# One reloaded factor rounded and split two places sooner at the turn of the pairs (gated linear attention and bilinear GLU, one Trainium2 core)

## The chip, the core and the metric

The kernel runs on one core of one Trainium2 chip. The metric is the device time of one execution in microseconds (us). Before the change it is 596.92 us, the median of 3 runs (596.91 to 597.69).

The engines are named as in the profile: PE multiplies matrices, PEld loads the stationary operand, DVE is VectorE, ACT is ScalarE, POOL is GpSimd, SP issues most of the transfers. Each engine runs its own instructions in the order in which the program emits them; between engines there are semaphores.

## What is computed

```python
x = A_x                                   # 2048 tokens, width 512
g = sigmoid((x * gate_w).sum(-1))
a = linear_attention(x, A_wqkv) @ A_wo    # 32 heads of 16, phi(t) = where(t > 0, t + 1, exp(t)) + 1e-6
b = ((x @ B_w_gate) * (x @ B_w_up)) @ B_w_down     # inner width 1792
return g * a + (1 - g) * b
```

All data are float32. The kernel gets that precision out of PE by splitting each operand into a rounded high part and a low part (`hi`, `lo = src - hi`) and by making three matmuls of each product: high by high, high by low, low by high. A split is one ACT instruction (the rounding copy) and one DVE instruction (the subtraction), and the DVE one waits for the ACT one.

## The kernel before

The 2048 tokens are worked in two pairs of two chunks of 512. A first phase makes the key-value sums over all tokens; then come 32 units, 16 for each pair. A unit (`unit`, line 484) takes one 128-column block of the gate and up weights (or of the query weights) and makes the two by two blocks of the result with seven products instead of eight (a Strassen-like scheme). Each product (`product`, line 502) is six matmuls: two halves of the contraction, three matmuls each. The seven products go in the order 2, 3, 4, 1, 5, 6, 7, into four PSUM banks called Y, X, R and S (`bY`, `bX`, `bR`, `bS` in the profile).

The factor of product `i` on the token side is `xc[i]`, a pair of tiles, high and low: `xc1h` and `xc1l` for product 1, a part of `xbh` and `xbl` for product 5, `xc6h` and `xc6l` for product 6, a part of `xah` and `xal` for product 7. These factors belong to a pair of chunks, so they have to be renewed between unit 15, the last of the first pair, and unit 16, the first of the second. Factors 2, 3 and 4 of the second pair are made early and kept elsewhere. Factors 1, 5, 6 and 7 are reloaded by `reload` (line 489): right after the last product of unit 15 that reads factor `i`, SP issues a 512 KB load of the summed x into the low tile, and the split of it (ACT rounds it into the high tile, DVE subtracts in place) is put off to a place of unit 16. The trace calls the ACT instruction `xc1h<-xc1l` and the DVE one `xc1l<-xc1l,xc1h`; for factor 5 they are `xbh<-xbl` and `xbl<-xbl,xbh`.

What sets the order of the work is written out by hand. A unit calls named places in between its products, in the order of `PLACES` (line 43): high, low, e, m, c, d, t, s, r, end. `later(n, place, fn)` (line 418) puts a function on the list of a place, `do(n, place)` (line 421) runs the list in the order in which it was filled. For unit 16 the stretch that matters is, in program order (lines 510 to 540):

- product 2 into Y; ACT empties Y into `m`; place high
- product 3 into X; DVE writes R from X and `m`; places low and e; the down-projection jobs of this point (none in unit 16)
- product 4 into Y; ACT empties it into `cross[0]`; places m and c; one down-projection job (six matmuls into `pdn`); place d
- the rounding of the next unit's weights (`wch`), then product 1 onto R; DVE makes `t` from R and `cross[0]`; place t
- product 5 onto X; DVE makes S from `t` and X; two jobs; place s; two jobs; product 6, place r, product 7

Before the change the splits of factors 1, 5, 6 and 7 stand at the places m, c, t and s of unit 16. At the places high and low of unit 16 the rounding and the subtraction of the last hidden tile of unit 15 are queued as well (lines 588 and 589; `xc4l<-cross` on ACT and `xc4l<-cross,xc4l` on DVE in the trace, because its buffer is a part of a tile that has become free). Line 589 is reached after `reload(1)`, so what `reload(1)` puts on the place low comes ahead of that subtraction in the list.

After the turn the order goes on without a break: attention units whose denominators take a way through DRAM (`den<-den`, `rb<-den`) and, at the end of the second pair, a second seven-product scheme for the down projection (`sa`, `sb`).

Of the kernel before, what the change touches and what calls it, by code (L numbers as in the profile page):

```python
# [42 lines left out]
PLACES = "high low e m c d t s r end".split()  # L43
# [5 lines left out]
)  # L49
STARTS = (0, 4, 5, 7)  # L50
MOST = (2, 3, 2, 2)
Q_AFTER = ((5, 9), (0, 3))


# [9 lines left out]
def gated_mix(ctx: ExitStack, tc, xt, xp, x, wqkv, wq, wq_add, wo, wgu, wgu_add, wdn, gate_w, out):  # L64
# [12 lines left out]
    def act(dst, src, func=AF.Copy, **kw):  # L77
        pin(nc.scalar.activation(dst, src, func, **kw))  # L78

    def tt(dst, a, b, op):  # L80
        pin(nc.vector.tensor_tensor(dst, a, b, op=op))  # L81
# [12 lines left out]
    def mm3(dst, lhs, rhs, start, stop, on=False, late=0, part=range(3)):  # L94

        (lh, ll), (rh, rl) = lhs, rhs
        three = ((lh, rh), (ll, rh), (lh, rl)) if late else ((lh, rh), (lh, rl), (ll, rh))
        for i in part:
            mm(dst, *three[i], start=start and i == 0, stop=stop and i == 2, skip_group_check=on)

    def dma(dst, src):
        tc.keep_in_program_order(nc.sync.dma_start(dst, src))
# [45 lines left out]
    order = []  # L148
    for pair, after in enumerate(Q_AFTER):
        for f in range(NF):  # L150
# [3 lines left out]
    units = len(order) // NPAIR  # L154
# [11 lines left out]
    def w_add(n):  # L166

        if n < len(order):
            _, kind, m = order[n]
            act(raws[n][:, 3:5], raws[n][:, 0:1].to_broadcast([P, 2, 2 * P]))  # L170
            act(raws[n][:, 5:7], raws[n][:, 0:2], scale=-1.0)
            dma_add(raws[n][:, 2:7], (wgu_add if kind == "f" else wq_add)[m])
# [3 lines left out]
    def w_high(n):  # L176
        if n < len(order):
            wcs[n] = [const.tile([P, 7, 2 * P], F32R, tag=f"wc{v}", name=f"wc{v}", bufs=2) for v in "hl"]
            for a, b in PARTS:
                act(wcs[n][0][:, a:b], raws[n][:, a:b])  # L180

    def w_low(n, part):
        if n < len(order):
            a, b = PARTS[part]
            tt(wcs[n][1][:, a:b], raws[n][:, a:b], wcs[n][0][:, a:b].bitcast(F32), ALU.subtract)
# [19 lines left out]
    with tc.tile_pool(name="p1", bufs=2, reuse_waits="tile") as p1:  # L205
# [11 lines left out]
        for t in range(2 * CH // P):  # L217
            c, i = divmod(t, CH // P)
# [180 lines left out]
    def put(*some):  # L399
        for one in some:  # L400
            if one.home:
                spare.append(one.r)
            else:
                live.remove(one)

    def two(name):
        return [Buf(name + v, True) for v in "hl"]
# [10 lines left out]
    def later(n, place, fn):  # L418
        at.setdefault((n, place), []).append(fn)

    def do(n, place):
        for fn in at.pop((n, place), []):
            fn()
        if n >= units:
            clock[0] += 1
            advance(dve=MOST[0], act=MOST[1])

# [13 lines left out]
    def advance(**most):  # L441

        for i, job in enumerate(jobs):
            for k, chain in enumerate(job.chains):
                while chain:
                    kind, lead, gap, fn, ready = chain[0]
                    if lead < i or clock[0] < job.free[k] or not ready() or not most.get(kind, 1):
                        break
                    if kind in most:
                        most[kind] -= 1  # L450
                    fn()
                    job.free[k] = clock[0] + gap
                    chain.pop(0)
# [3 lines left out]
    def down(k, all_=False):  # L457

        owed[0] += k
        for _ in range(owed[0]):  # L460
            if not jobs or jobs[0].apart and passed[0] == passed[1] and not all_:
                break
            waits = [stage for chain in jobs[0].chains for stage in chain]
            if waits and not all_:
                break
            for kind, lead, gap, fn, ready in waits:
                assert ready(), clock
                fn()
            job = jobs.pop(0)
            owed[0] -= 1  # L470
            clock[0] += 1
            job.mms()
            passed[1] = passed[0]
            advance(dve=MOST[2], act=MOST[3])
            if job.after:
                job.after()
        if not jobs:
            owed[0] = 0


    def share(n):
        return SECOND[n - units] if n >= units else FIRST[n]

    def unit(n, quad=None, sign=None, og=None):

        wh, wl = wcs.pop(n)
        bank = {t: psum.tile([P, CH], F32, tag=t, name=f"b{t}") for t in "YXRS"}

        def reload(i):
            if n + 1 == units and i not in xsum:  # L490
                spare.extend(v[:, k] for v in xc[i] for k in range(2))
            elif n + 1 == units:
                hi, lo = xc[i]
                dma(lo.bitcast(F32), xsum[i])

                def split_there():
                    act(hi, lo.bitcast(F32))
                    tt(lo, lo.bitcast(F32), hi.bitcast(F32), ALU.subtract)

                later(units, {1: "m", 5: "c", 6: "t", 7: "s"}[i], split_there)  # L500

        def product(i, to, start=False):
            for k in range(2):
                ks = slice(k * P, (k + 1) * P)
                x = [v.r for v in kept[i, k]] if n >= units and i not in xsum else [v[:, k] for v in xc[i]]
                mm3(bank[to], (wh[:, SLOT[i], ks], wl[:, SLOT[i], ks]), x, start and k == 0, k == 1, not start)
            passed[0] += 1
            reload(i)

        turned = [sign is not None and c != sign for c in range(2)]  # L510
        m2 = Buf("m2")
        product(2, "Y", True)
        act(m2.f, bank["Y"])
        do(n, "high")
        product(3, "X", True)

        tt(bank["R"], bank["X"], m2.f, ALU.subtract)
        put(m2)
        do(n, "low")
        do(n, "e")  # L520
        many = share(n)
        down(many[0])
        cross = [Buf(f"cross{c}") for c in range(2)]
        product(4, "Y")
        act(cross[0].f, bank["Y"], scale=-1.0 if turned[0] else 1.0)
        do(n, "m")
        do(n, "c")
        down(many[1])
        do(n, "d")
        if n:  # L530
            w_high(n + 1)
        w_add(n + 2)
        product(1, "R")
        t = Buf("t")
        tt(t.f, bank["R"], cross[0].f, ALU.subtract if turned[0] else ALU.add)
        if n:
            w_low(n + 1, 0)
        do(n, "t")
        product(5, "X")
        tt(bank["S"], t.f, bank["X"], ALU.subtract)  # L540
        put(t)
        act(cross[1].f, bank["X"], scale=-1.0 if turned[1] else 1.0)
        down(many[2])
        if quad:
            quad(1, 0, cross[0].f)
            put(cross[0])
        if n:
            w_low(n + 1, 1)
        do(n, "s")
        down(many[3])  # L550
        w_low(n + 1, 2)
        if quad:
            quad(0, 1, cross[1].f)
            put(cross[1])
        product(6, "R")

        def hidden(c, to):
            tt(cross[c].f, bank[to], cross[c].f, ALU.mult)
            if og and c == 0:
                tt(cross[c].f, cross[c].f, og.f, ALU.mult)  # L560

        if quad:
            quad(1, 1, bank["R"])
        else:
            hidden(1, "R")
            if sign is None:
                h = {c: two("h") for c in range(2)}
                act(h[1][0].r, cross[1].f)
        do(n, "r")
        product(7, "S")  # L570
        if quad:
            quad(0, 0, bank["S"])
            return
        if sign is not None:
            hidden(0, "S")
            return cross

        def high(c):
            act(h[c][0].r, cross[c].f)

        def low(c):
            tt(h[c][1].r, cross[c].f, h[c][0].f, ALU.subtract)
            put(cross[c])

        if n + 1 < len(order):
            hidden(0, "S")
            low(1)
            later(n + 1, "high", lambda: high(0))
            later(n + 1, "low", lambda: low(0))
        else:  # L590
            low(1)
            hidden(0, "S")
            high(0)
            low(0)
        return h
# [610 lines left out]
```

## Time and profile before

| | us |
|---|---|
| median of 3 runs | 596.92 |
| lowest and highest run | 596.91, 597.69 |
| the profiled execution, its own time | 596.23 |
| span of that execution, first to last instruction | 594.5 |
| PE busy in the span | 587.7 |

The profile is that of one execution. Busy times of the engines overlap each other. A matmul of 128x512 is shown with 0.39 us, but the matmuls are pipelined, and the next one starts some 0.23 us after it. In a timeline a row gives the start, the duration, the engine, the line, the operation, the tiles (written before the arrow, read behind it), the shape and, in brackets, the idle time of the engine before it and what ended that. Nearly all instructions are recorded at the lines of small helpers: L72 is any matmul, L78 any ACT activation, L81 any DVE operation on two tensors, L102 any load or store by SP, L105 any adding transfer by POOL. They are told apart by their tiles.

### The profile page before, as it was taken

What the parts mean: (1) busy time and instruction counts of PE and PEld (TensorE: products, weight loads), DVE (VectorE), ACT (ScalarE), POOL (GpSimd) and SP (SyncE); (2) the same over time, 40 slices, a digit from 0 to 9 for tenths busy, and PEclk for the clock granted to TensorE, in tenths of its full rate; (3) what the DMA queues carried; (4) which work ended last, traced back from release to release, by engine and by line L of the source; (5) the groups of instructions that cost most, each with busy time, mean ns of one, the idle gap of its engine ahead of it and who ended that gap; (6) DMA issues with size and microseconds to landing.
All of it is one profiled execution on the core that took longest, in us unless ns stands there. A gap on an engine that the chain in (4) does not pass through costs nothing.

```text
span 594.5 us, 7844 instructions
## 1 busy us (share of the span) xinstructions
PE 587.7 (99%) x2634; PEld 482.8 (81%) x2634; DVE 476.8 (80%) x772; ACT 348.3 (59%) x620; POOL 82.6 (14%) x103
## 2 busy tenths in 40 slices
PE   9999999999999999999999999999999999999997
PEld 6888888888888888888888788887788888888886
DVE  6877896775576788776888757996898999699996
ACT  3856775677538454663564646448957855655620
POOL 0011100100111000001110043203104202401000
PEclk9999999999999999999999999999999999999999
DMA  9477947978777967558694879769877957733003
GB/s 305 156 205 129 287 98 220 226 205 241 218 153 173 291 165 209 134 142 185 145 235 126 234 181 238 208 148 237 181 202 125 242 110 175 142 73 62 1 0 142
DMA packets 63064, 103.29 MB, mean 174 GB/s; under 512 B 8288, under 2 KB 33376, under 8 KB 63008
## 3 DMA queue, kind: packets, MB, share of 16 engines
q1 hardware_dynamic: 49568, 68.72, 35.2%
q0 software_dynamic: 13168, 33.56, 32.7%
q10 hardware_dynamic: 288, 0.52, 0.3%
q8 instruction: 20, 0.33, 0.2%
q14 instruction: 20, 0.16, 0.1%
HBM read 86.77 MB, written 16.66 MB: 174 GB/s over the span
## 4 chain that ended last, share of the span: by engine, by line
PE 96%; DMA 2%; DVE 0%; ACT 0%; issue 0%; SPq 0%; DVEq 0%
PE pdn L72 18%; PE bR L72 14%; PE bY L72 14%; PE bX L72 14%; PE pk L72 7%; PE gt L72 7%; PE bS L72 7%; PE sa L72 7%; PE sb L72 6%; DMA rb<-den 1%; PE warm L72 1%; PE pw L72 0%; PE pkv L72 0%; DMA den<-den 0%; DVE xc1l L81 0%
## 5 line engine op out<-in xcount | busy, mean ns | idle before, releaser
L81 DVE TENSOR_TENSOR wcl<-wr,wch 128x512 fp32r<-128x512 f32 (+1 forms) x96 | 73.5, 774 | 1.6 <-ACT wch L78 1.5
L81 DVE TENSOR_TENSOR acc<-pdn,acc 128x512 f32<-128x512 f32 (+1 forms) x71 | 47.4, 681 | 21.4 <-PE pdn L72 21.0
L78 ACT ACTIVATE wch<-wr 128x512 fp32r<-128x512 f32 (+1 forms) x96 | 60.3, 694 | 3.0 <-DMA wr<-in_wgu_add 3.0
L105 POOL DMA_DIRECT2D wr<-in_wgu_add x28 | 27.0, 964 | 236.6 <-ACT wr L78 149.7
L78 ACT ACTIVATE hh<-cross 128x512 fp32r<-128x512 f32 x29 | 18.2, 627 | 50.1 <-DVE cross L81 50.1
L72 PE MATMUL pdn<-hl,dh 128*128 128x512 f32 (+1 forms) x113 | 43.8, 387 | 0.0
L72 PE MATMUL pdn<-hh,dl 128*128 128x512 f32 (+1 forms) x113 | 43.7, 387 | 0.0
L72 PE MATMUL pdn<-hh,dh 128*128 128x512 f32 (+1 forms) x113 | 43.7, 387 | 0.0
L81 DVE TENSOR_TENSOR bR<-bX,m 128x512 f32<-128x512 f32 x32 | 22.3, 697 | 22.9 <-PE bX L72 22.7
L78 ACT ACTIVATE m<-bY 128x512 f32<-128x512 f32 x32 | 19.1, 598 | 36.3 <-PE bY L72 36.0
L78 ACT ACTIVATE cross<-bY 128x512 f32<-128x512 f32 x32 | 19.1, 596 | 36.2 <-PE bY L72 36.2
L72 PE MATMUL bX<-xbh,wch 128*128 128x512 f32 x96 | 37.3, 389 | 0.0
L72 PE MATMUL bX<-xbl,wch 128*128 128x512 f32 x96 | 37.3, 389 | 0.0
L72 PE MATMUL bX<-xbh,wcl 128*128 128x512 f32 x96 | 37.3, 389 | 0.0
L78 ACT ACTIVATE wr<-wr 128x512 f32<-128x512 f32 x64 | 36.5, 620 | 1.3 <-DMA wr<-in_wgu 1.3
L81 DVE TENSOR_TENSOR t<-bR,cross 128x512 f32<-128x512 f32 x32 | 22.0, 688 | 15.2 <-PE bR L72 8.5
L78 ACT ACTIVATE cross<-bX 128x512 f32<-128x512 f32 x32 | 19.0, 593 | 25.7 <-DVE bS L81 25.7
L72 PE MATMUL bR<-xc1l,wch 128*128 128x512 f32 x64 | 25.0, 391 | 0.8 <-DVE xc1l L81 0.8
L72 PE MATMUL bR<-xc1h,wch 128*128 128x512 f32 x64 | 25.2, 393 | 0.3 <-ACT xc1h L78 0.3
L72 PE MATMUL bR<-xc6h,wch 128*128 128x512 f32 x64 | 25.1, 392 | 0.0
L72 PE MATMUL bS<-xah,wch 128*128 128x512 f32 x64 | 25.0, 391 | 0.0
L72 PE MATMUL bR<-xc1h,wcl 128*128 128x512 f32 x64 | 24.9, 389 | 0.0
(385 smaller groups left out, 1732.6 us busy)
## 6 DMA issues: line engine op xcount, KB each, us to landing
wr<-in_wgu_add POOLq DMA_DIRECT2D x28, 640.0 KB, 6.9
wr<-in_wgu SPq DMA_DIRECT2D x28, 384.0 KB
xraw<-in_x SPq DMA_DIRECT2D x16, 256.0 KB
wdr<-in_wdn SPq DMA_DIRECT2D x16, 256.0 KB
terms<-zq SPq DMA_DIRECT2D x16, 256.0 KB
zt<-terms SPq DMA_DIRECT2D x16, 256.0 KB
rb<-den SPq DMA_DIRECT2D x16, 256.0 KB
ws<-in_wdn SPq DMA_DIRECT2D x30, 128.0 KB
```

The costliest lines, as they stand in the source:

```text
L72: tc.keep_in_program_order(nc.tensor.matmul(*args, **kw))
L78: pin(nc.scalar.activation(dst, src, func, **kw))
L81: pin(nc.vector.tensor_tensor(dst, a, b, op=op))
L105: tc.keep_in_program_order(nc.gpsimd.dma_start(dst, src, accum_op=ALU.add))
```

## The change

The places of the four reloaded factors are moved into a table, `RELOAD`, that gives one number for the rounding and one for the subtraction: the index of the place in `PLACES`, counted from the place high of unit 16.

```diff
+RELOAD = {1: (1, 1), 5: (4, 4), 6: (6, 6), 7: (7, 7)}
...
                 hi, lo = xc[i]
                 dma(lo.bitcast(F32), xsum[i])
 
-                def split_there():
+                def high():
                     act(hi, lo.bitcast(F32))
+
+                def low():
                     tt(lo, lo.bitcast(F32), hi.bitcast(F32), ALU.subtract)
 
-                later(units, {1: "m", 5: "c", 6: "t", 7: "s"}[i], split_there)
+                for fn, at_ in zip((high, low), RELOAD[i]):
+                    m, one = divmod(at_, len(PLACES))
+                    later(units + m, PLACES[one], fn)
```

Index 4 is c, 6 is t and 7 is s, so factors 5, 6 and 7 keep their places. Index 1 is low, where it was m (index 3): one ACT instruction and one DVE instruction, once in the kernel, stand two places sooner. No instruction, transfer or buffer is added or removed, and the load of the factor is issued at the point where it was.

## The prediction

> **What bounds the kernel now.** I read the page's head first, then the list of who waited for whom, for PE alone, over the whole span.
>
> ```profile
> span 594.5 us, 7844 instructions
> PE 587.7 (99%) x2634; PEld 482.8 (81%) x2634; DVE 476.8 (80%) x772; ACT 348.3 (59%) x620; POOL 82.6 (14%) x103
> ```
> ```profile
> PE warm L72 <- DVE xc1h L128: 1.3, 1, 1.3
> PE bR L72 <- DVE xc1l L81: 0.8, 1, 0.8
> PE sb L72 <- ACT sb L78: 0.7, 1, 0.7
> PE bR L72 <- ACT xc1h L78: 0.3, 1, 0.3
> ```
>
> PE is the bound: it works 587.7 us of 594.5, and the list holds only four waits. The one for `warm` is the start of the kernel. Two of the other three are waits of product 1 for the two halves of `xc1`, the very split that moves. Next the chain that ended last, in order of time, around the turn, and PE's own instructions there.
>
> ```profile
> 330.90 1.06 ACT xc1h L78
> ...
> 331.99 1.24 DVE xc1l L81
> ...
> 333.26 1.43 PE bR L72 x5
> 334.69 1.36 PE bX L72 x6
> ```
> ```profile
> 331.34 0.39 PE L72 MATMUL pdn<-hl,xal 128*128 128x512 f32 x1
> 332.00 0.50 PE L72 MATMUL bR<-xc1h,wch 128*128 128x512 f32 x1 [0.27 <-ACT xc1h L78]
> 333.26 0.50 PE L72 MATMUL bR<-xc1l,wch 128*128 128x512 f32 x1 [0.76 <-DVE xc1l L81]
> 333.60 0.40 PE L72 MATMUL bR<-xc1h,wcl 128*128 128x512 f32 x1
> ...
> 334.53 0.39 PE L72 MATMUL bX<-xbh,wch 128*128 128x512 f32 x1
> 334.76 0.39 PE L72 MATMUL bX<-xbl,wch 128*128 128x512 f32 x1
> 334.98 0.39 PE L72 MATMUL bX<-xbh,wcl 128*128 128x512 f32 x1
> ...
> 335.89 0.39 PE L72 MATMUL pdn<-hh,dh 128*128 128x512 f32 x1
> ```
>
> The chain leaves PE here: it runs through ACT's rounding and DVE's subtraction of `xc1` and comes back to product 1. The reader should not add up the idle times in brackets (0.27 + 0.76), for they are measured against matmuls recorded as 0.39 us long, while undisturbed ones follow each other every 1.36 / 6 = 0.227 us. From the start at 331.34 to the one at 335.89 lie 13 such steps, 2.95 us undisturbed; the trace has 4.55. **The turn costs PE 1.60 us**: 0.43 before the first matmul of product 1 (332.00 where 331.57 was due), 1.03 before the second (333.26 where 332.23 was due), and the rest after the restart, since the step from 333.26 to 333.60 is 0.34 instead of 0.227.
>
> **The change, step by step.** It adds and removes nothing; it moves two instructions. What stands where they go is in ACT's and DVE's timelines.
>
> ```profile
> 328.24 0.62 ACT L78 ACTIVATE xc4l<-cross 128x512 fp32r<-128x512 f32 x1
> 330.41 0.60 ACT L78 ACTIVATE cross<-bY 128x512 f32<-128x512 f32 x1 [1.54 <-PE bY L72]
> 330.90 1.05 ACT L78 ACTIVATE xc1h<-xc1l 128x1024 fp32r<-128x1024 f32 x1
> 331.85 1.05 ACT L78 ACTIVATE xbh<-xbl 128x1024 fp32r<-128x1024 f32 x1
> ```
> ```profile
> 329.12 0.70 DVE L81 TENSOR_TENSOR bR<-bX,m 128x512 f32<-128x512 f32 x1 [0.76 <-PE bX L72]
> 329.73 0.68 DVE L81 TENSOR_TENSOR xc4l<-cross,xc4l 128x512 fp32r<-128x512 f32 x1
> 331.99 1.22 DVE L81 TENSOR_TENSOR xc1l<-xc1l,xc1h 128x1024 fp32r<-128x1024 f32 x1 [1.58 <-ACT xc1h L78]
> 333.13 1.22 DVE L81 TENSOR_TENSOR xbl<-xbl,xbh 128x1024 fp32r<-128x1024 f32 x1
> ```
>
> *The rounding of `xc1`, now behind `xc4l<-cross`.* ACT is idle for 1.54 us before `cross<-bY`, which waits for PE. The rounding starts at about 328.8 (an ACT instruction follows its predecessor some 0.1 us before that one's end: 330.41 to 330.90 for one of 0.60) and ends at 328.8 + 1.05 = 329.85. It fits into the idle time with 0.5 us to spare, so `cross<-bY`, which is now queued behind it, still starts at 330.41. Cost on the path: nothing while that cover holds; without it ACT would pay 0.95 us, the step from 330.90 to 331.85.
>
> *The subtraction, now behind `bR<-bX,m` and ahead of `xc4l<-cross,xc4l`.* It starts at 329.89 (0.04 after the rounding, as 331.99 stands to 331.95) and ends at 329.89 + 1.22 = 331.11. DVE's idle 1.58 us covers it. The hidden tile's subtraction slips behind it, to some 331.0 to 331.7; its tile is read by the jobs only from 340.65 on, where the trace has `pdn<-xc4l,xal`, so nobody waits.
>
> ```profile
> 340.65 0.84 PE L72 MATMUL pdn<-xc4l,xal 128*128 128x512 f32 x3
> ```
>
> *Product 1.* Both halves of `xc1` are there by 331.11, the due time of its first matmul is 331.57. The whole 1.60 us goes: the six run from 331.57, and product 5 is due at 331.57 + 6 x 0.227 = 332.93.
>
> *What is late next: `xbl`.* ACT rounds `xbh` right after `cross<-bY`, so at 330.90 instead of 331.85, and ends at 331.95. DVE, free by 331.7, subtracts from 331.99 to 333.21. The second matmul of product 5 reads `xbl` and is due at 333.16. Priced like the restart above: 333.21 + 0.04 until PE starts, + 0.34 until the next one, gives 333.59 for the third matmul, due at 331.57 + 8 x 0.227 = 333.39. **A loss of 0.21 us**, and everything behind it starts 1.39 us sooner than before. The trace has no such wait now (`xbl` is done at 334.35, its matmul starts at 334.76), so I take bounds: 0 below, if the weight load costs nothing where I let it cost 0.04 + 0.34; above, if the load of `xbl` were the limit. It was there at 331.85 at the latest, when its rounding began with no wait. Rounding from then on, the subtraction would be done at 332.90 + 0.04 + 1.22 = 334.16, the third matmul would go at 334.54, and the loss would be 1.15.
>
> *Are the loads there?* The trace shows no landings of SP's loads, so I bound them by bytes.
>
> ```profile
> 319.30 0.33 SPq L102 DMA_DIRECT2D xc1l<-xsum  x1
> 320.66 0.33 SPq L102 DMA_DIRECT2D xbl<-xsum  x1
> ```
> ```profile
> 320.00:324.00 4.00, 4.00 (x19) 3.32 (x18) 3.11 (x6) 2.01 (x4) 0.87 (x1) 1.00 0.83 236
> 324.00:328.00 4.00, 4.00 (x20) 3.30 (x19) 3.90 (x7) 0.88 (x2) 0.00 (x0) 1.00 1.00 190
> 328.00:332.00 4.00, 3.73 (x17) 2.76 (x15) 1.67 (x4) 2.46 (x5) 0.00 (x0) 1.00 1.00 393
> ...
> 336.00:337.00 1.00, 1.00 (x6) 0.83 (x5) 0.45 (x2) 0.66 (x1) 0.87 (x1) 1.00 0.00 0
> ```
> ```profile
> wr<-in_wq_add POOLq DMA_DIRECT2D x1, 640.0 KB, 8.5
> ```
>
> The last column is GB/s. In 320 to 324 and 324 to 328 some 944 + 760 = 1704 KB move. The two loads are 524 KB each, and POOL's adding transfer of that time is 655 KB. With all of that transfer counted ahead, `xc1l` is complete (1179 KB) at about 325.2, well before 328.8, and `xbl` (1703 KB) at 328.0, well before 330.90, if one queue's loads finish in turn. [...]
>
> *Does the gain last to the end?* The transfer engines are empty at 336 to 337 (share 0.00), so no backlog from before the turn holds anything later up, and what follows is issued by an order that starts 1.39 us sooner. ACT moves up by only 0.95 at first (the step that is taken out ahead of `xbh`), but it waits for PE again before the one remaining stall, four times and up to 5.5 us in the waits between 333 and 394, and from the first of these on it runs the whole 1.39 ahead:
>
> ```profile
> ACT m L78 <- PE bY L72: 13.6, 4, 5.5
> ```
>
> *Sum.* -1.60 + 0.21 = -1.39 us, of the profiled execution's 596.23 (span 594.5 and 1.73 around it): 594.84. The median of the runs is 0.69 above that execution; the difference taken off the median is 596.92 - 1.39 = **595.5 us**.
>
> **The rivals.**
>
> *Nothing is late next.* `xbl` costs nothing, the gain is 1.60: 595.3. For it speaks that the miss is only 0.05 us (333.21 to 333.16); against it, that the wait ended at 333.26 shows the restart cost that I charge.
>
> *`xbl` is bound by its load.* The upper bound above: gain 1.60 - 1.15 = 0.45, 596.5. For it speaks the full traffic (share 1.00) from 324 on, against it the byte count.
>
> *Given back at the next stall.* PE's `sb` wait, 0.7 us in the first list, hangs on transfers.
>
> ```profile
> 396.90 8.05 DMA rb<-den
> ```
> ```profile
> 396.30 2.51 SPq L102 DMA_DIRECT2D rb<-den  x4
> ```
> ```profile
> 396.79 0.86 POOL L105 DMA_DIRECT2D wr<-in_wgu_add  x1 [9.45 <-DVE bS L81]
> ```
> ```profile
> 400.00:404.00 4.00, 4.00 (x19) 3.30 (x19) 3.04 (x5) 1.84 (x5) 0.00 (x0) 1.00 1.00 242
> ```
>
> If `rb` landed at its old time, PE would come to the wait 1.39 us sooner and wait 0.7 + 1.39: all is lost, 596.9. For it speaks that the transfer takes 8.05 us with the engines full (1.00). Against it: they ran empty at 336, so the landing follows its issue, and the issue follows the program.
>
> *The load of `xc1` is late, and the change costs time.* At the new place ACT waits for the load with `cross<-bY` and `xbh` behind it. The trace of before only proves that the load was there at 330.90. Landing then, `xc1` is no sooner than before; `cross<-bY` starts at 331.85, `xbh` at 332.34; DVE does `xc1l` (331.99), the hidden tile it did before (333.13), and `xbl` from 333.74 to 334.96. The third matmul of product 5 goes at 334.96 + 0.38 = 335.34 instead of 334.98: 0.36 slower, 597.3. The same steps with an earlier landing break even at about 330.55, so it decides from there. Against it: the byte count has it there five microseconds sooner.
>
> *The order of two transfers turns round.* `rb` is issued at 396.30, POOL's adding transfer at 396.79. Should that transfer gain 0.49 us on `rb`, its 655 KB go first, 2.7 us at the 242 GB/s of 400 to 404, and the `sb` wait grows by as much: 596.92 - 1.39 + 2.7 = 598.2. For it speaks only the small distance. Against it: both are released by the same shifted order.
>
> That the change doesn't do what it says I rule out but for the late load: the two instructions are the only ones that move.
>
> **How the numbers follow.** Chances: forecast 0.66; nothing late next 0.10; `xbl` bound by its load 0.04; given back 0.09; late load 0.05; turned order 0.06. A measurement of this kernel tells some 0.2% from no change, 1.2 us. The forecast's 1.39 is just over that, the first rival's 1.60 as well; the runs differ by more than the margin (596.91 to 597.69), so I give the forecast 4 in 5 to come out faster by over 0.2% (0.53) and the first rival 9 in 10 (0.09): faster 0.62. Within 0.2% are what these two leave (0.13 + 0.01) and the second, third and fourth (0.04 + 0.09 + 0.05): 0.32. Slower by over 0.2%, from 598.1 on, is the last one: 0.06. The forecast's own range, with both ends of the `xbl` term that leave it the likeliest (0 and 0.4) and a third of a microsecond for the runs, is 595.0 to 596.0. The whole range reaches from the first rival less that third and a little more for an `sb` wait that shrinks, 594.8, to the third rival with its spread, 597.1; it leaves out the turned order and the late load's upper part.
>
> **What the changed profile would show.** Right: `xc1h<-xc1l` stands on ACT at about 328.8 and `cross<-bY` still at 330.4; `xc1l<-xc1l,xc1h` stands on DVE at 329.9, ahead of the hidden tile's subtraction; PE's list of waits has no `xc1` any more and a new one of some 0.2 us or less for `xbl`; the first matmul of `pdn` after product 5 starts at 334.5 instead of 335.9; the `sb` wait is still 0.7 and comes at 406.1. Wrong: an idle ACT ahead of `xc1h` that a transfer ended; an `xbl` wait near a microsecond; an `sb` wait of 2 us or more; or a shift of 1.39 at 340 that is no longer there at the end.

## The result, and the profile after

| | before | after |
|---|---|---|
| median of 22 runs each (us) | 596.91 | 595.38 |
| lowest and highest run | 595.80, 598.38 | 594.42, 597.46 |
| ratio after to before | | 0.9981 (95% interval 0.9973 to 0.9989) |
| the profiled execution, its time and its span | 596.23, 594.5 | 595.02, 593.3 |

The ratio is a gain of 1.1 us (0.7 to 1.6), the medians lie 1.53 apart; 1.39 was predicted. All lines of the changed kernel are one higher than before (the table takes a line), so L73 is what L72 was.

First PE's waits in the changed kernel, the whole list: how long in total, how often, the longest.

```profile
PE warm L73 <- DVE xc1h L129: 1.3, 1, 1.3
PE sb L73 <- ACT sb L79: 0.2, 1, 0.2
PE pk L73 <- ACT wkh L79: 0.2, 1, 0.2
```

Both waits for `xc1` are gone, and none for `xbl` is listed in their place. The new one for `pk` belongs to the loads of the first microseconds, and `sb` waits for less than the 0.7 us of before; neither is near the change, and both come back below. Now PE at the turn.

```profile
331.93 0.39 PE L73 MATMUL pdn<-hl,xal 128*128 128x512 f32 x1
332.15 0.39 PE L73 MATMUL bR<-xc1h,wch 128*128 128x512 f32 x1
...
333.51 0.39 PE L73 MATMUL bX<-xbh,wch 128*128 128x512 f32 x1
333.85 0.50 PE L73 MATMUL bX<-xbl,wch 128*128 128x512 f32 x1
334.19 0.40 PE L73 MATMUL bX<-xbh,wcl 128*128 128x512 f32 x1
...
335.11 0.39 PE L73 MATMUL pdn<-hh,dh 128*128 128x512 f32 x1
```

From the matmul ahead of product 1 to the one behind product 5 it is 335.11 - 331.93 = 3.18 us, where it was 4.55 and 2.95 would be undisturbed. Product 1 follows without a gap. What is left sits at `xbl`: the two steps from 333.51 to 334.19 are 0.68 us instead of 0.454. The list of waits doesn't show it, because it counts only from the recorded end of a matmul on; the starts do. ACT and DVE there:

```profile
328.83 0.62 ACT L79 ACTIVATE xc4l<-cross 128x512 fp32r<-128x512 f32 x1
329.35 1.05 ACT L79 ACTIVATE xc1h<-xc1l 128x1024 fp32r<-128x1024 f32 x1
330.99 0.60 ACT L79 ACTIVATE cross<-bY 128x512 f32<-128x512 f32 x1 [0.60 <-PE bY L73]
331.49 1.05 ACT L79 ACTIVATE xbh<-xbl 128x1024 fp32r<-128x1024 f32 x1
```
```profile
329.70 0.70 DVE L82 TENSOR_TENSOR bR<-bX,m 128x512 f32<-128x512 f32 x1 [0.76 <-PE bX L73]
330.43 1.23 DVE L82 TENSOR_TENSOR xc1l<-xc1l,xc1h 128x1024 fp32r<-128x1024 f32 x1
331.57 0.69 DVE L82 TENSOR_TENSOR xc4l<-cross,xc4l 128x512 fp32r<-128x512 f32 x1
332.57 1.23 DVE L82 TENSOR_TENSOR xbl<-xbl,xbh 128x1024 fp32r<-128x1024 f32 x1 [0.31 <-ACT xbh L79]
```

The rounding of `xc1` fills ACT's idle time (0.60 of the 1.54 us is left), `cross<-bY` still waits for PE and not for ACT, and the subtraction stands ahead of the hidden tile's. All of it is 0.59 us later than in the prediction's trace, because this execution came to the turn 0.59 later.

### The profile page after: what moved, and what is told of

The parts are those of the page before. It is cut to its first block, busy times and chain, and to the rows that moved or that the text cites. A ratio compares the mean times of both kernels' runs of the same rounds, so it can differ in the third digit from the quotient of the medians.

```text
span 593.3 us, 7844 instructions
## 1 busy us (share of the span) xinstructions
PE 587.9 (99%) x2634; PEld 483.2 (81%) x2634; DVE 476.6 (80%) x772; ACT 348.5 (59%) x620; POOL 82.5 (14%) x103
## 4 chain that ended last, share of the span: by engine, by line
PE 96%; DMA 2%; ACT 0%; DVE 0%; issue 0%; SPq 0%; DVEq 0%
PE pdn L73 18%; PE bR L73 14%; PE bY L73 14%; PE bX L73 14%; PE pk L73 8%; PE gt L73 7%; PE bS L73 7%; PE sa L73 7%; PE sb L73 6%; DMA rb<-den 1%; DMA wraw<-in_wqkv 1%; PE pw L73 0%; PE pkv L73 0%; DMA den<-den 0%; DVE rb L85 0%
## 5 line engine op out<-in xcount | busy, mean ns | idle before, releaser
L79 ACT ACTIVATE wch<-wr 128x512 fp32r<-128x512 f32 (+1 forms) x96 | 60.4, 693 | 2.4 <-DMA wr<-in_wgu_add 2.4
L73 PE MATMUL pdn<-hh,dl 128*128 128x512 f32 (+1 forms) x113 | 43.8, 387 | 0.0
L73 PE MATMUL pdn<-hh,dh 128*128 128x512 f32 (+1 forms) x113 | 43.7, 387 | 0.0
L73 PE MATMUL pdn<-hl,dh 128*128 128x512 f32 (+1 forms) x113 | 43.7, 387 | 0.0
L73 PE MATMUL bX<-xbl,wch 128*128 128x512 f32 x96 | 37.5, 390 | 0.0
L73 PE MATMUL bX<-xbh,wch 128*128 128x512 f32 x96 | 37.4, 389 | 0.0
L73 PE MATMUL bX<-xbh,wcl 128*128 128x512 f32 x96 | 37.4, 389 | 0.0
L73 PE MATMUL bR<-xc6h,wch 128*128 128x512 f32 x64 | 25.1, 392 | 0.0
L73 PE MATMUL bR<-xc1h,wch 128*128 128x512 f32 x64 | 25.0, 391 | 0.0
L73 PE MATMUL bS<-xah,wch 128*128 128x512 f32 x64 | 25.0, 391 | 0.0
L73 PE MATMUL bR<-xc1h,wcl 128*128 128x512 f32 x64 | 24.9, 389 | 0.0
L73 PE MATMUL bR<-xc6l,wch 128*128 128x512 f32 x64 | 24.9, 389 | 0.0
```

What stands on the lines that cost most here:

```text
L73: tc.keep_in_program_order(nc.tensor.matmul(*args, **kw))
```

## The experiments

Each profile is cut into three: P, the start of the last matmul ahead of product 1; the turn, from there to the first matmul behind product 5; and the rest, to the end of the span. All are us from the rows of each trace; "later waits" are PE's waits behind the turn. Each ratio is to runs of the kernel before that were taken in one set with it (their medians are 596.31 to 596.92). A profile is that of one run, which need not be a typical one: for "the change, again" and "two places later" it is the slowest of twelve (597.47 and 602.32), for "load last of four, split at m" the fastest of six (597.96).

| kernel | P | turn | rest | later waits | median | ratio to before (95%) |
|---|---|---|---|---|---|---|
| before | 331.34 | 4.55 | 258.6 | 0.7 | 596.91 | |
| before, again | 331.93 | 4.57 | 259.0 | 1.1 | (597.24, one run) | |
| the change | 331.93 | 3.18 | 258.2 | 0.2 | 595.38 | 0.9981 (0.9973 to 0.9989) |
| the change, again | 331.72 | 3.19 | 260.9 | 1.9 | 595.08 | 0.997 (0.9955 to 0.9985) |
| rounding only | 331.92 | 3.19 | 259.4 | 1.2 | 595.15 | 0.9961 (0.9947 to 0.9976) |
| both factors early | 331.20 | 2.94 | 259.4 | 1.4 | 594.95 | 0.9956 (0.9939 to 0.9973) |
| two places later | 331.94 | 8.51 | 260.2 | 1.3 | 600.74 | 1.0047 (1.0027 to 1.0067) |
| load behind all, split at low | 331.36 | 9.55 | 259.0 | 1.0 | 601.77 | 1.0085 (1.0068 to 1.0102) |
| load behind all, split at m | 331.62 | 9.85 | 257.7 | none | 602.27 | 1.0107 (1.0074 to 1.014) |
| load last of four, split at low | 331.13 | 9.28 | 259.2 | 1.3 | 601.64 | 1.0085 (1.0055 to 1.0115) |
| load last of four, split at m | 331.36 | 6.41 | 258.4 | 0.6 | 601.80 | 1.0082 (1.005 to 1.0113) |
| load third of four, split at low | 331.39 | 7.36 | 258.4 | 0.4 | 598.24 | 1.0029 (1.0012 to 1.0046) |
| change, add later | 331.39 | 3.22 | 258.7 | 0.8 | 595.10 | 0.9978 (0.9963 to 0.9993) |
| both early, add later | 331.84 | 2.95 | 258.9 | 1.0 | 594.93 | 0.9967 (0.9955 to 0.998) |

### The two kernels once more

No edit. Are the turn and the `sb` wait the same in another execution?

> The changed kernel once more, for a second profile of it beside the kernel before. The turn is measured from the start of the last matmul of the down-projection job ahead of product 1 to the start of the first matmul of the job behind product 5: 4.55 us before the change, 2.95 undisturbed. Theory (the stall of product 1 is gone and a restart before the xbl matmul of product 5 takes its place): 3.17 +- 0.05 again, ratio to the kernel before 0.9977. The wait of sb near 406 us, 0.7 before the change, 0.2 in the first profile of the change: if it follows the landing of rb and not the change, it lies anywhere from 0 to 1 us; if the change itself shortens it, it is 0.2 again and 0.7 again in the kernel before. Rival (the gain is a matter of this one profile): the turn is over 4 us.

> The kernel before once more, for a second profile of it. Theory: turn 4.55 us again. The wait of sb near 407 us: 0.7 again if it belongs to the order of the program, anything from 0 to 1 us if it follows the landing of rb.

The turn is the same to 0.02 us, before (4.55, 4.57) and after (3.18, 3.19). The `sb` wait is not: 0.7 and 1.1 before, 0.2 and 1.9 after. It hangs on the second of the four transfers of `rb`: DVE works on `rb` when that transfer is there, then ACT on `xc4l` and on `sb`, a tile of the second scheme, and PE waits for `sb`. The chain of waits of the changed kernel, in the first profile and in the second, shows what it follows (start, duration):

```profile
396.14 7.57 DMA rb<-den
```
```profile
395.94 9.23 DMA rb<-den
```

Before, the same transfer took 8.05 (wait 0.7) and, again, 8.48 (1.1). The wait is the transfer's duration less some 7.4 us in all four. The first `rb` transfer is issued 60.4 us behind the end of the turn in all four as well (395.54 - 335.11 in the first profile of the change): the issue moves with the turn, the duration does not follow it. In the second execution of the change it had a further price. Its stretches of 2 us; behind the busy times of the engines stand PE's granted clock, the share of the transfer engines and GB/s:

```profile
406.00:408.00 2.00, 0.32 (x1) 0.30 (x2) 2.00 (x4) 2.00 (x4) 0.00 (x0) 1.00 0.86 285
408.00:410.00 2.00, 2.00 (x6) 1.59 (x5) 2.00 (x4) 2.00 (x5) 0.00 (x0) 0.52 0.66 191
410.00:412.00 2.00, 2.00 (x7) 1.53 (x6) 0.77 (x2) 2.00 (x5) 1.04 (x2) 0.63 0.83 249
412.00:414.00 2.00, 2.00 (x11) 1.65 (x10) 0.45 (x1) 2.00 (x5) 2.00 (x5) 1.00 0.79 124
```

After this wait of 1.9 us PE's clock was granted at about half for some 3.4 us (an estimate from these rows: (0.48 + 0.37) x 2 us short of the full clock, divided by a half), so that the wait cost more than its own length. The table's columns for the rest and the later waits explain what is left: in the profiles in which the clock held after the turn, the rest less its later waits is 257.7 to 258.2 us, whatever stood at the turn. In this one it is 259.0.

### Only the rounding earlier

```diff
-RELOAD = {1: (1, 1), 5: (4, 4), 6: (6, 6), 7: (7, 7)}
+RELOAD = {1: (1, 3), 5: (4, 4), 6: (6, 6), 7: (7, 7)}
```

> Only the rounding of factor 1 stands at the place low; its subtraction stays at m, where it was. Theory (ACT's rounding, queued behind cross<-bY, was what was late, and DVE had nothing between low and m but the hidden tile's subtraction): that subtraction runs first, xc1l follows it and is done some 0.5 us later than in the change, 0.2 us ahead of its matmul; turn 3.2 us, at most 3.3, ratio to the kernel before 0.998. Rival (the subtraction has to be early too): product 1 waits for xc1l again, turn 3.7 us or more, half of the gain or less.

DVE's timeline of this kernel:

```profile
330.31 0.68 DVE L82 TENSOR_TENSOR xc4l<-cross,xc4l 128x512 fp32r<-128x512 f32 x1
330.91 1.22 DVE L82 TENSOR_TENSOR xc1l<-xc1l,xc1h 128x1024 fp32r<-128x1024 f32 x1
332.57 1.23 DVE L82 TENSOR_TENSOR xbl<-xbl,xbh 128x1024 fp32r<-128x1024 f32 x1 [0.44 <-ACT xbh L79]
```

The subtraction comes after the hidden tile's and ends at 332.13, 0.47 later than in the change, and still ahead of its matmul (332.38); `xbl` starts at the same 332.57. The turn is 3.19. The whole gain is the ACT instruction's; that the DVE one moves too is without effect here.

### Both factors early

```diff
-RELOAD = {1: (1, 1), 5: (4, 4), 6: (6, 6), 7: (7, 7)}
+RELOAD = {1: (1, 1), 5: (1, 1), 6: (6, 6), 7: (7, 7)}
```

> Factor 5 is rounded and split at the place low as well, behind factor 1. Theory (xbl is late by 0.2 us only because its rounding stands behind cross<-bY, and its load is there by 329.7): ACT does both roundings ahead of cross<-bY, which starts some 0.26 us later than it could and holds up nobody; no wait at all is left in the turn, 2.95 to 3.0 us, 0.2 us less than the change, some 1.6 us less than the kernel before (ratio 0.9973). Rival (the load of factor 5 limits xbl): an idle ACT ahead of xbh that a transfer ended, turn 3.2 us or more.

ACT and PE of this kernel:

```profile
328.62 1.05 ACT L79 ACTIVATE xc1h<-xc1l 128x1024 fp32r<-128x1024 f32 x1
329.57 1.05 ACT L79 ACTIVATE xbh<-xbl 128x1024 fp32r<-128x1024 f32 x1
330.52 0.58 ACT L79 ACTIVATE cross<-bY 128x512 f32<-128x512 f32 x1
```
```profile
332.79 0.39 PE L73 MATMUL bX<-xbh,wch 128*128 128x512 f32 x1
333.01 0.39 PE L73 MATMUL bX<-xbl,wch 128*128 128x512 f32 x1
333.24 0.39 PE L73 MATMUL bX<-xbh,wcl 128*128 128x512 f32 x1
```

The two roundings follow each other with no wait for a load, the matmuls of product 5 keep their step, and the turn is 2.94: nothing is left to gain there. So the 0.23 us of the change was `xbh`'s place behind `cross<-bY`, and the load of factor 5 is there by 329.57.

### Two places later than before

```diff
-RELOAD = {1: (1, 1), 5: (4, 4), 6: (6, 6), 7: (7, 7)}
+RELOAD = {1: (5, 5), 5: (4, 4), 6: (6, 6), 7: (7, 7)}
```

> The split of factor 1 stands at the place d, two places later than before the change, behind factor 5's split and behind the down-projection job's addition. Theory (the time is set by where the two instructions stand in ACT's and DVE's order): ACT rounds xbh first (330.90 to 331.95 in the time of the kernel before), then xc1h to 332.90; DVE does xbl, the addition, and xc1l to 334.94; product 1 goes on at 334.98 and product 5 finds xbl ready; turn 6.25 us, 1.7 more than before the change, ratio 1.0028. Rival (PE waits for the load or for something else, and the place counts little): turn near 4.55, ratio 1.000.

PE at the turn of this kernel, and one of its stretches:

```profile
331.94 0.39 PE L73 MATMUL pdn<-hl,xal 128*128 128x512 f32 x1
333.55 0.49 PE L73 MATMUL bR<-xc1h,wch 128*128 128x512 f32 x1 [1.22 <-ACT xc1h L79]
335.59 0.80 PE L73 MATMUL bR<-xc1l,wch 128*128 128x512 f32 x1 [1.55 <-DVE xc1l L82]
336.19 0.63 PE L73 MATMUL bR<-xc1h,wcl 128*128 128x512 f32 x1
336.61 0.63 PE L73 MATMUL bR<-xc1h,wch 128*128 128x512 f32 x1
...
340.45 0.63 PE L73 MATMUL pdn<-hh,dh 128*128 128x512 f32 x1
```
```profile
336.00:338.00 2.00, 2.00 (x6) 1.52 (x6) 0.00 (x0) 1.25 (x2) 0.87 (x1) 0.50 0.03 11
```

The order did what the theory said: the second matmul of product 1 starts 3.65 us after P, 3.64 were expected (334.98 less 331.34). The size in this profile did not: from there on the matmuls follow each other every 0.43 us instead of 0.227, at a clock of 0.50, and the turn is 8.51 instead of 6.25. But this is the slowest of twelve runs, and they fall into two groups: seven took 600.67 to 602.32 at a mean granted clock of 0.993 to 0.997, five took 597.78 to 598.40 at 1.000. Those five are 1.0 to 1.6 us above the kernel before (596.78), near the 1.7 that were expected. The waits of the engines were worked out rightly; what the sum left out is that PE's clock may fall during or after them, here to 0.50.

### A late load

What if the load is late for the new place? Two pairs of kernels and a single one issue the load of factor 1 later. The first pair ("load behind all" in the table) issues it at the place high of unit 16, with the split at low and at m. In the trace that is behind the loads of the other three factors and one load of weights (`wr<-in_wgu`); the loads of `wph` and `wpl` still come behind it:

```diff
-                dma(lo.bitcast(F32), xsum[i])
+                if i == 1:
+                    later(units, "high", lambda: dma(lo.bitcast(F32), xsum[i]))
+                else:
+                    dma(lo.bitcast(F32), xsum[i])
```

> The load of factor 1 is issued behind all other loads of the turn (at the place high of unit 16) and so lands late, at a time L after 330.9; the split stands at low, as in the change. Theory of the late load (ACT takes its instructions in order, so the waiting rounding holds up cross<-bY and xbh): ACT sits idle ahead of xc1h until a transfer ends it, cross<-bY and xbh come behind it, xbl is late for product 5 as well; the turn is 0.4 us longer (0.3 to 0.5) than with the same late load and the split at m. Rival (an early place is never worse): the two turns are equal.

> The same late load, with the split at m, as before the change. Theory of the late load: cross<-bY runs at its old time, ahead of the waiting rounding; xc1h waits for the transfer, xbl is ready in time for product 5; the turn is 0.4 us shorter than with the split at low, and both are longer than 4.55 by as much as the load lands after 330.9.

The second pair issues it behind the loads of the other three factors, the single kernel behind those of two (`i == 6` for `i == 7`, the split at low):

```diff
-                dma(lo.bitcast(F32), xsum[i])
+                if i != 1:
+                    dma(lo.bitcast(F32), xsum[i])
+                if i == 7:
+                    dma(xc[1][1].bitcast(F32), xsum[1])
```

> The load of factor 1 is issued behind the three other factors' loads (after factor 7's), the split stands at low, as in the change. By bytes it lands near 330.7 in the time of the kernel before, late by under 2 us, so that PE's clock, which fell to half in the runs with longer waits, should hold. Theory of the late load: ACT waits for the transfer ahead of xc1h, cross<-bY and xbh come behind it, xbl is some 0.4 us late for product 5; turn 4.75 us, 0.2 more than with the same load and the split at m. Rival (an early place is never worse): turn equal to that of the split at m, or shorter.

> The same order of loads, with the split at m. Theory of the late load: the load is there when cross<-bY is done, or some tenths later, the turn is 4.55 us as in the kernel before (up to 0.3 more if it lands after 330.9), some 0.2 less than with the split at low.

> The load of factor 1 is issued behind those of factors 5 and 6 (third of four), the split stands at low. It should land somewhere between 328 and 332 in the time of the kernel before. P is the start of the last matmul ahead of product 1 (331.34 there), L the start of xc1h on ACT if a transfer ended ACT's wait for it. Theory of the late load: turn = (L - P) + 5.34 us for L - P over -1.3, against the larger of 4.55 and (L - P) + 4.96 with the split at m; so a landing at P would cost 0.4 to 0.8 us against the kernel before, and one 0.8 us ahead of P breaks even. If the transfer ends no wait of ACT, the turn is that of the change, 3.18. Rival (an early place is never worse than a late one): the turn stays at (L - P) + 4.96 or below. If PE's clock falls to half, as after the waits of 2.8 us and more, the turn tells nothing.

ACT in the kernel with the load third of four, and in the one with the load last of four and the split at m:

```profile
328.29 0.62 ACT L79 ACTIVATE xc4l<-cross 128x512 fp32r<-128x512 f32 x1
332.16 1.06 ACT L79 ACTIVATE xc1h<-xc1l 128x1024 fp32r<-128x1024 f32 x1 [3.25 <-DMA xc1l<-xsum]
333.12 0.58 ACT L79 ACTIVATE cross<-bY 128x512 f32<-128x512 f32 x1
333.60 1.05 ACT L79 ACTIVATE xbh<-xbl 128x1024 fp32r<-128x1024 f32 x1
```
```profile
330.43 0.60 ACT L79 ACTIVATE cross<-bY 128x512 f32<-128x512 f32 x1 [1.54 <-PE bY L73]
332.78 1.06 ACT L79 ACTIVATE xc1h<-xc1l 128x1024 fp32r<-128x1024 f32 x1 [1.75 <-DMA xc1l<-xsum]
333.74 1.04 ACT L79 ACTIVATE xbh<-xbl 128x1024 fp32r<-128x1024 f32 x1
```

The mechanism is there: with the split at low the waiting rounding holds `cross<-bY` back from about 330.4 to 333.12, with the split at m it doesn't. Its price, the 0.4 us that `xbl` would be late, no run isolates. The pair with the load last of four missed its expectations, turns of 4.75 and 4.55: the load landed at 333.83 and 332.78, not near 330.7, and the turns are 9.28 and 6.41. In the profile with the split at m PE's clock held (granted 1.00 in every stretch from 320 to 342), and the turn is what the sum of the last expectation, applied to it afterwards, gives: (332.78 - 331.36) + 4.96 = 6.38, measured 6.41. In the profiles of all four others PE's clock fell to about half (granted 0.50 to 0.55 in the lowest stretch of 2 us). With the load third of four the sum is (332.16 - 331.39) + 5.34 = 6.11 and the turn 7.36; at half clock the matmuls come so slowly, one every 0.43 us, that `xbl` is in time, and the surplus is the clock's. A load that is late costs time with the split at low as well: that kernel's ratio to the one before is 1.0029 (1.0012 to 1.0046). With the load behind all, the turns of the pair are 9.55 and 9.85, against an expected 0.4 the other way; the loads landed 2.96 and 3.11 us behind P, and PE's clock was at half for some 3.4 us in the one and 6.8 in the other (the same estimate, from granted clocks of 0.70, 0.50 and 0.95 from 336 to 342 and of 0.52, 0.50, 0.50 and 0.77 from 334 to 342), so the comparison tells nothing of the place. Whether an early place is worse than a late one under a late load stays open.

The pair also shows how the loads of one queue share the transfer engines. Traffic of the kernel with the load last of four and the split at m:

```profile
320.00:324.00 4.00, 4.00 (x19) 3.31 (x18) 3.11 (x6) 2.02 (x4) 0.86 (x1) 1.00 0.60 148
324.00:328.00 4.00, 4.00 (x20) 3.30 (x19) 3.90 (x7) 0.86 (x2) 0.00 (x0) 1.00 0.89 205
328.00:332.00 4.00, 3.75 (x17) 2.78 (x15) 1.67 (x3) 1.48 (x3) 0.00 (x0) 1.00 1.00 356
332.00:334.00 2.00, 0.11 (x1) 0.11 (x1) 0.13 (x1) 1.22 (x2) 0.00 (x0) 1.00 1.04 402
```

The four loads and POOL's adding transfer are 2752 KB. Up to 332.78, when the load of factor 1 ends ACT's wait, 592 + 820 + 1424 + 314 = 3150 KB have moved, so some 400 KB that were issued behind it had moved before it was complete. That does not mean that a later load overtook it. The kept traces also hold the updates of each load's semaphore, 16 to a load, which the views above don't list. In this kernel the last of them come at 324.3 for factor 5, 329.5 for factor 6, 331.0 for factor 7 and 332.76 for factor 1, and at 333.7 for the load of weights issued next, whose first update stands at 332.4 already. So a load begins to land before the one ahead of it has ended, but the four loads were complete in their order of issue, here and in each of the 14 profiles (in that of before at 322.7, 325.8, 330.7 and 331.9 for factors 1, 5, 6 and 7).

### The adding transfer later

What makes the second transfer of `rb` take 7.6 to 9.2 us? POOL's adding transfer is issued 0.49 us behind the first of the four, and so just ahead of the second (396.04 against 396.15 in the change). In unit 20 it is put off:

```diff
-        w_add(n + 2)
+        if n == 20:
+            later(n, "s", lambda: w_add(n + 2))
+        else:
+            w_add(n + 2)
```

> The changed kernel, with the two copies of w_add and its adding transfer of unit 20 put off from the place d to the place s, so that POOL issues it 1 to 2 us behind rb instead of 0.49. Theory (the sb wait is what rb's transfer loses to the adding transfer, and its spread from 0.2 to 1.9 us is the spread of that): rb takes 7.4 us or less, the sb wait is 0 to 0.2 us, the time from the end of the turn to the end of the span is 257.9 to 258.1 us, and the median is some 1 us below the changed kernel's, ratio to the kernel before 0.996. Rival (rb is slow by itself): transfer of 7.6 to 9.2 us and a wait of 0.2 to 1.9 us as before.

> The same, with the split of factor 5 at low too. Theory: turn 2.95 us, sb wait 0 to 0.2 us, no wait of PE over 0.3 us left behind the start; another 0.2 us below the one before, ratio to the kernel before 0.9955. Rival: the gain of the turn comes back as a longer sb wait, the time from the end of the turn to the end of the span is over 258.5 us.

In the first of the two kernels SP issues the first transfer of `rb` at 395.02 and the second at 395.62, and POOL the adding transfer at 397.33. PE's list of waits, DVE's second use of `rb`, and a piece of the chain that ended last:

```profile
PE warm L73 <- DVE xc1h L129: 1.3, 1, 1.3
PE bY L73 <- DVE wcl L82: 0.8, 1, 0.8
PE pk L73 <- ACT wkh L79: 0.5, 1, 0.5
```
```profile
401.99 0.69 DVE L85 SCALAR_TENSOR_TENSOR rb<-ph,rb 128x512 f32<-128x512 f32 x1
```
```profile
397.33 9.75 DMA wr<-in_wgu_add
```

DVE uses the second transfer at 401.99 without a wait, at most 6.4 us after its issue; by the updates of its semaphore it was there at 399.4, after 3.8 us (3.8 in the other kernel too). The `sb` wait is gone in both kernels. So what `rb` lost, it lost to the adding transfer beside it. But that transfer now takes 9.75 us (9.99 in the other kernel) where it took 7.5 to 9.1 in the profiles of before and of the change, and it is issued later; the next unit's weights are late, and PE waits for them, 0.8 and 1.0 us. Of the expectation the mechanism held and the gain did not: the rest is 258.7 and 258.9 us, no better than the others. The second kernel's median, 594.93, is the lowest of the table by a hair, and its 12 runs lie closer together (593.55 to 595.45) than the 22 of the change (594.42 to 597.46). But its ratio to the kernel before, 0.9967 (0.9955 to 0.998), is not the lowest and overlaps with that of the change, so that it is better than the change is not shown; that the turn has no wait left is.

## Why the prediction was right, point by point

- **The turn.** Predicted 4.55 - 1.60 + 0.21 = 3.16, measured 3.18 and 3.19. Product 1's stall went as a whole, and it was the rounding's place that made it: the kernel that moves the rounding alone has the same turn.
- **What is late next.** `xbl` was charged 0.21 us, and the steps at 333.51 to 334.19 have 0.68 - 0.454 = 0.23. That it was `xbh`'s place behind `cross<-bY`, not its load, is shown by the kernel with both factors early (turn 2.94). This settles the first two rivals: something is late next, and it isn't the load.
- **The cover.** 0.5 us of ACT's idle time was to be left ahead of `cross<-bY`, 0.60 is. The hidden tile's subtraction slipped as forecast, and nobody waited for it.
- **The loads.** The byte count had the load of `xc1` complete at about 325.2 and that of `xbl` at 328.0. It assumed that the loads of one queue finish in turn, which they did in every profile, and it counted POOL's adding transfer ahead of them, which was too careful. The prediction said that the trace shows no landings of SP's loads; the views don't, but by the semaphores' updates in the kept traces the two were complete at 322.7 and 325.8 before the change, and that of `xc1` at 323.5 after it, 5.8 us ahead of its rounding. No load ended a wait of ACT in the change, and the rival of the late load had no ground here.
- **The way to the end.** The rest less PE's later waits didn't change (257.9 before, 258.0 after), so the gain of the turn is not used up by the order of the work. The `sb` wait was the weak step: the prediction took 0.7 us as a constant, and it varies from one execution to the next, from 0.2 to 1.9 us in two of the same kernel. The two first profiles, of before and after, differ by 1.2 us in their spans, but by 1.37 at the turn, 0.5 at `sb`, and 0.59 the other way at the start. The rival "given back", a longer wait because PE comes sooner, needed a landing that stays where it was; instead `rb`'s issue moves with the turn in all four profiles of the two kernels. Whether the transfer takes longer on average after the change can't be told from so few: waits of 0.7 and 1.1 before, 0.2, 1.9, 1.2 and 1.4 in the four with the shorter turn (the change twice, the rounding only, both factors early).
- **The two slower rivals.** In the late load the order of events was right and the price is open. In the turned order the competition between `rb` and the adding transfer is real, but the distance between the issue of the first `rb` transfer and that of the adding transfer stays, as the prediction argued (396.30 and 396.79 before, 395.54 and 396.04 after). The prediction looked at the wrong one of the four, though: the transfer that `sb` hangs on is the second, and its issue (396.90) stood behind that of the adding transfer already before the change, so that there was no order to turn round.
- **The size in the end.** 1.39 us predicted; 1.1 (0.7 to 1.6) by the ratio, 1.8 (0.9 to 2.7) in the second set of runs. That the median of 595.38 lies only 0.12 from the predicted 595.5 is in part luck, for the median of the kernel before alone moves between 596.31 and 596.92 from set to set. The runs spread over 2.6 us before and 3.0 after; in the profiles the `sb` wait is the largest part of the spread, which is why 0.2% is about all that can be told here.

## What to carry to other kernels

In an order written out by hand, look for the engine that is idle just ahead of a late chain, and for the earliest instruction of the chain that could run there: here one rounding of 1.05 us, moved into 1.54 us of idle time, took away a stall of 1.60, and the subtraction behind it needed no move. Then work out what is due next with the shift already in it; the second factor, in time by 0.41 us before, became the new limit. Take starts of matmuls, not listed waits, to measure such a stretch, and compare a small change by the stretch that it touches, for the rest of this kernel varies by more than the gain.

## What the runs showed of the hardware

In six of the 14 profiles PE's clock fell to about half during or after waits that I had priced as plain waiting. It fell after a single wait of 1.9 us (`sb` in the change, again; granted clock 0.52), after two with one matmul between them of 1.5 and 0.8 us (load third of four, 0.50), of 3.7 and 0.8 (load behind all, split at low, 0.50) and of 3.4 and 0.8 (load last of four, split at low, 0.55), in the first of two of 3.8 and 0.5 us (load behind all, split at m, 0.50) and in the second of two of 1.22 and 1.55 us (two places later, 0.50). It was low for some 3.4 us, in the last two cases for twice that, by the estimate from stretches of 2 us that stands above; matmuls then start every 0.43 us instead of 0.227 (two places later). It did not fall after the 0.27 and 0.76 us of the kernel before (granted 1.00 from 332 to 338), nor after a single wait of 1.4 us (both factors early, 1.00 from 400 to 420), nor, in one execution, after 2.1 and 0.8 us (load last of four, split at m, 1.00 from 332 to 342). So the idle time alone doesn't decide it, and one program goes both ways: of the twelve runs of "two places later" five have a mean granted clock of 1.000, one has 0.997 and six have 0.993 or 0.994. One stretch of 3.4 us at half clock takes 1.7 of some 600 us, 0.003 of the mean, so by this estimate these are runs with none, one and two of them. What decides it no run here shows.
